# An attention and feed-forward kernel: TensorE's planned waits of the first stages filled with matmuls of the identity

## The chip, the cores and the metric

The kernel runs on one core of one Trainium2 chip. The metric is the device time of one execution in microseconds (us), as the median of several runs. Engines: PE (TensorE, matmuls, with its weight loads shown as PEld), DVE (VectorE), ACT (ScalarE), POOL (GpSimd) and SP (SyncE, which only issues transfers here). PE writes its results to PSUM, which this kernel uses as eight banks of 128 partitions by 2 KB.

## The reference

Linear attention with a decay per head runs in blocks of 64 positions for 4 batches, 8 heads, 768 positions and a head size of 64. Its output, laid out as 3072 rows of 512, goes through a feed-forward layer with SiLU.

```python
for b in range(nb):                                   # blocks of 64 positions
    intra = np.einsum('bhic,bhjc->bhij', qb, kb) * Dmask[None]   # lam ** (i - j), lower triangle
    intra = np.einsum('bhij,bhjd->bhid', intra, vb)
    inter = np.einsum('bhid,bhde->bhie', qb * lam_pow[None], kv_state)
    out[:, :, sl] = intra + inter
    kb_dec = kb * rev_pow[None]
    kv_state = lam_block[None, :, None, None] * kv_state + np.einsum('bhsd,bhse->bhde', kb_dec, vb)
...
h = x @ w_in                                          # 3072 x 512 times 512 x 2048
g = h * (1.0 / (1.0 + np.exp(-h)))
return g @ w_out                                      # 3072 x 2048 times 2048 x 512
```

## The kernel before

**Units and sets.** A unit is 128 positions (two blocks of 64) of one batch: 24 units, 6 along the sequence for each of 4 batches. Two units make a set, and q, k and v of a set are loaded by three transfers of 512 KB each from SP (`load_set`). The four first sets hold units 0 and 1 of one batch; later ones hold one unit of two batches.

**Attention of a set.** k is cast to bf16 (tile `kq`), q is scaled by the decay on its way to bf16 (`kq`, with `lam_q`), and v is scaled too (`vd`, with `lam_v`). Queries and keys are turned: in the first four sets by eight transposes on PE for each of k and q, which are matmuls against `ident` into the PSUM tile `tr` (L455), copied to SBUF as `kqT`; in later sets by a transposing DMA. PE then makes the state's increments (`d_ps`, L476 or L664) and the scores (`st_ps`, L527 or L674). DVE multiplies the scores by the triangle (`st`). PE makes the outputs from `st` and `vd` (`x_ps`, L551 or L696) and adds the part of the state (L556 or L704), after which `x_ps` is copied to `xt`, the feed-forward input, already transposed.

**Feed-forward.** The first product (`product1`, L843) makes `h_ps` from `w_in_bf` and `xt` in groups of eight matmuls of 128x256 or four of 128x512. SiLU on ACT (L852) turns `h_ps` into `g`. The second product is plain for eight units (L874) and otherwise a seven-product scheme with sums of operands made on DVE and POOL (L1087; L957 for the last group of the first product). Results go to DRAM from ACT's queue and, at the end, from SP's. The weights are loaded by POOL's queue in eight transfers, each held back until a load of k has landed (the copy to `gate`, L330).

**The planner.** No order is written out by hand. Every step is a `Task` with a key (its urgency), a planned duration on each engine that may run it, the tasks that it depends on, and the buffers that it uses (`Buf`, by pools; `bank` is a PSUM bank, eight of them). `Planner.order` plays a clock over the engines: at each event it gives every free engine the ready task with the least key whose buffers are free, and books `free[e] = now + t.on[e]`. A buffer's slot goes back to the end of its pool's list when its last user's planned end is reached, and a task takes its slot from the front of the list (`pop(0)`). Transfers are planned with rates (`SMALL`, `WIDE` and so on). What comes out is a list of tasks in planned order, and the kernel then issues the instructions in this order. So the order on each engine is fixed when the kernel is built; on the chip, each engine runs its own list in order, and semaphores hold an instruction until what it needs is there. If a planned duration is wrong, the order stays and the waits move.

`tile_of` makes a tile in the SBUF or PSUM slot that the planner chose; a new tile in a slot brings, at its first write, a wait for the last users of the tile that had the slot before.

`ident`, the identity matrix in bf16, is made by POOL at the start (L255, L256); the transposes of L455 use it.

## Time and profile before

| what | value |
|---|---|
| median of 3 runs | 208.56 us (208.56 to 210.06) |
| the profiled execution | 209.46 us, its span 207.8 us |
| PE busy | 187.7 us, 90% of the span, 2446 matmuls |
| DVE, ACT, POOL busy | 135.6, 110.4, 65.7 us |
| PE busy from 0 to 22.9 us | 10.74 us |
| PE busy from 28.61 us to the end | 172.10 of 179.19 us |
| DMA share, 0 to 22.9 us | 1.01 |

The span runs from the first to the last instruction of one execution; what lies around it makes the rest of that execution's time. Line numbers are those of the kernel before. A row of the timeline gives start, length, engine, line, operation, output from inputs, tile and shape, and in brackets the idle time before it with the instruction that ended it. A row of waits gives who waited for whom, in total, how often, and the longest. The ends of matmuls are modelled.

### The profile page before, as it was taken

To read this page: it belongs to the slowest core of one execution; us is meant where nothing else is said; L and a number is where in the kernel's file an instruction comes from. 1 tells how busy PE (TensorE), PEld (TensorE's weight loads), DVE (VectorE), ACT (ScalarE), POOL (GpSimd) and SP (SyncE) were. 2 spreads that over 40 slices of the span, in tenths; PEclk is the share of its full clock that TensorE was granted. 3 is DMA by queue.
4 is the path that set the end of the run, shared out by engine and by line. 5 is a ranking of instruction groups with operands and counts; after the bars stand their busy time and mean duration, and the time that the engine had idled before them with its cause. 6 is when DMAs were issued, how large, how long until landed. Compare 5 with 4: busy or idle time off the path is not lost.

```text
span 207.8 us, 5721 instructions
## 1 busy us (share of the span) xinstructions
PE 187.7 (90%) x2446; PEld 133.3 (64%) x2464; DVE 135.6 (65%) x234; ACT 110.4 (53%) x200; POOL 65.7 (32%) x86
## 2 busy tenths in 40 slices
PE   0258999999999999999997999997999999999993
PEld 0146679776667655544586745675476778888882
DVE  6469563787770186719999693899965854755511
ACT  3634666875444273457553286572646473666220
POOL 6222310623240042307666430477213222222200
PEclk9999999999999999999999999999999999999999
DMA  3999999999999999999979999911501110103303
GB/s 101 295 256 258 237 270 238 248 201 204 236 261 231 183 229 226 208 246 222 177 149 200 219 223 218 229 39 54 104 3 50 54 50 0 54 0 101 104 32 121
DMA packets 88617, 33.92 MB, mean 163 GB/s; under 512 B 67088, under 2 KB 87568, under 8 KB 88592
## 3 DMA queue, kind: packets, MB, share of 16 engines
q1 hardware_dynamic: 79232, 23.60, 56.2%
q0 software_dynamic: 4224, 4.19, 12.1%
q10 hardware_dynamic: 5136, 5.77, 8.3%
q8 instruction: 19, 0.31, 0.6%
q14 instruction: 6, 0.05, 0.1%
HBM read 27.27 MB, written 6.29 MB: 162 GB/s over the span
## 4 chain that ended last, share of the span: by engine, by line
PE 85%; DVE 7%; DMA 3%; ACT 2%; issue 1%; POOL 0%; DVEq 0%; POOLq 0%
PE h_ps L843 33%; PE o_ps L1087 21%; PE o_ps L874 13%; PE h_ps L957 6%; DMA raw<-in_k_dram 3%; PE tr L455 3%; PE x_ps L704 2%; DVE st L319 2%; PE d_ps L664 1%; PE x_ps L696 1%; DVE w_out_bf L319 1%; PE st_ps L674 1%; DVE kq L319 1%; PE x_ps L551 1%; PE d_ps L476 1%
## 5 line engine op out<-in xcount | busy, mean ns | idle before, releaser
L843 PE MATMUL h_ps<-xt,w_in_bf 128*128 128x256 bf16 (+1 forms) x441 | 75.8, 322 | 2.6 <-DVE xt L314 1.9
L852 ACT ACTIVATE g<-h_ps 128x512 bf16<-128x512 f32 x80 | 47.2, 595 | 33.8 <-PE h_ps L843 33.3
L843 PEld LDWEIGHTS <-w_in_bf 128*128 128x128 bf16 x448 | 43.7, 99 | 29.0 <-DVE xt L314 1.7
L319 DVE TENSOR_TENSOR st<-st_ps,tri 128x512 bf16<-128x512 f32 x32 | 20.3, 682 | 17.3 <-PE st_ps L674 17.2
L319 POOL TENSOR_TENSOR s<-g,s 128x512 bf16<-128x512 bf16 x16 | 19.2, 1198 | 39.2 <-DVE s L319 32.6
L874 PE MATMUL o_ps<-w_out_bf,g 128*128 128x512 bf16 x117 | 29.2, 379 | 0.7 <-issue 0.2
L1087 PEld LDWEIGHTS <-g 128*128 128x128 bf16 x256 | 24.9, 98 | 3.5
L1087 PEld LDWEIGHTS <-s 128*128 128x128 bf16 x192 | 18.7, 98 | 4.2 <-issue 1.4
L874 PEld LDWEIGHTS <-g 128*128 128x128 bf16 x128 | 12.1, 98 | 11.4
L319 DVE TENSOR_TENSOR osb<-o_ps,m 128x512 f32<-128x512 f32 (+1 forms) x15 | 8.7, 583 | 13.6 <-ACT m L312 8.8
L455 PE MATMUL tr<-ident,kq 128*128 128x128 bf16 x64 | 7.3, 264 | 10.3 <-POOL gate L330 6.9
L1087 PE MATMUL o_ps<-w_out_bf,s 128*128 128x256 bf16 x128 | 15.3, 273 | 1.2 <-DVE osb L319 1.2
L319 POOL TENSOR_TENSOR vd<-raw,lam_v 128x512 bf16<-128x512 f32 x10 | 13.8, 1386 | 6.5 <-DMA raw<-in_v_dram 6.3
L1087 PE MATMUL o_ps<-wsum,g 128*128 128x256 bf16 x128 | 15.1, 273 | 0.0
L1087 PE MATMUL o_ps<-w_out_bf,g 128*128 128x256 bf16 x128 | 14.8, 273 | 0.0
L312 ACT ACTIVATE xt<-x_ps 128x512 bf16<-128x512 f32 x15 | 9.2, 635 | 10.3 <-PE x_ps L704 6.1
L319 DVE TENSOR_TENSOR s<-g 128x512 bf16<-128x512 bf16 x16 | 10.5, 654 | 6.0 <-ACT g L852 4.0
L319 DVE TENSOR_TENSOR kq<-raw,lam_q 128x512 bf16<-128x512 f32 x17 | 13.7, 827 | 0.0
L455 PEld LDWEIGHTS <-kq 128*128 128x128 bf16 x64 | 5.3, 118 | 12.2 <-DVE kq L314 7.1
L312 ACT ACTIVATE m<-o_ps 128x512 f32<-128x512 f32 (+1 forms) x13 | 6.7, 514 | 11.7 <-PE o_ps L1087 11.7
L316 POOL CAST xe<-xf 64x256 bf16<-64x256 f32 (+1 forms) x8 | 6.5, 814 | 17.9 <-DVE xf L319 12.4
L312 ACT ACTIVATE osb<-o_ps 128x512 f32<-128x512 f32 (+1 forms) x12 | 6.7, 560 | 9.6 <-PE o_ps L874 4.8
(92 smaller groups left out, 245.6 us busy)
## 6 DMA issues: line engine op xcount, KB each, us to landing
raw<-in_k_dram SPq DMA_DIRECT2D x12, 512.0 KB, 7.6
raw<-in_q_dram SPq DMA_DIRECT2D x12, 512.0 KB, 8.3
raw<-in_v_dram SPq DMA_DIRECT2D x12, 512.0 KB, 7.0
out_dram<-osb ACTq DMA_DIRECT2D x20, 256.0 KB, 4.0
w_in_bf<-in_moe_w_in_dram POOLq DMA_DIRECT2D x4, 512.0 KB, 8.3
w_out_bf<-in_moe_w_out_dram POOLq DMA_DIRECT2D x4, 512.0 KB, 10.8
out_dram<-osb ACTq DMA_DIRECT2D x4, 128.0 KB, 1.8
out_dram<-osb SPq DMA_DIRECT2D x4, 128.0 KB, 1.7
```

The lines of the kernel that those rows point to most:

```text
L312: nc.scalar.activation(o, i, AF.Copy)
L316: nc.gpsimd.tensor_copy(o, i)
L319: (nc.vector if e == "DVE" else nc.gpsimd).tensor_tensor(o, a, b, op=op)
L455: nc.tensor.transpose(t[:, m, a], o.kq_of()[:, i, m, a], ident)
L476: nc.tensor.matmul(t[rp, m, :], lhsT=o.kq_of()[r, 0, m, a, p, :], rhs=o.vd_of()[r, 2 * m + p, a, :], start=m == 0 and a == 0, stop=True, s ...
L551: nc.tensor.matmul(t[rh, m], lhsT=o.vd_of()[r, 2 * m + h, a, :], rhs=o.st_of(h)[r, m, a], start=m == 0 and a == 0, stop=True, skip_group_c ...
L704: nc.tensor.matmul(x_of(c)[:, j, m, :], lhsT=o.xe[c].tile[:, (bs[0] + j) % 2, m, :], rhs=o.kqT_of()[:, 1, j, m, halves[c]], start=False, s ...
L843: nc.tensor.matmul(t[:, j, :], lhsT=w_in_bf[:, ko, 128 * (m1 + j):128 * (m1 + j) + 128], rhs=xt[gi].tile[:, ko, :], start=(ko == 0), stop= ...
L852: nc.scalar.activation(t[:, half * per:half * per + per], bank.tile, AF.Silu)
L874: nc.tensor.matmul(t, lhsT=g.tile[:, j, 128 * gp:128 * gp + 128], rhs=w_out_bf[:, ko, :], start=(ko == 0), stop=(ko == KO - 1))
L957: nc.tensor.matmul(t[:, j, :], lhsT=W[w]()[:, k2, f:f + 128], rhs=X(r)[:, k2, :], start=first and j == 0 and k2 == 0, stop=True, skip_grou ...
L1087: nc.tensor.matmul(t[:, i_, :], lhsT=src(j)[:, k2, 128 * r:128 * r + 128], rhs=W[w]()[:, 2 * j + k2, :], start=first and i_ == 0 and j == ...
```

## The change

The planner gets a `filler`, a function that makes a task of four matmuls of `ident` with `ident`, 128x128 each, into one PSUM bank. Nothing reads the result. Whenever, in the plan, PE is free between 1.7 and 30 us, finds no task to take, and more than two banks are free, it is given a filler: booked for 0.44 us before 6.0 us of the plan and for 0.22 us after. The filler takes the bank at the end of the list (`pop()`, the one freed last) and gives it back when its booked time is over. Because a filler occupies PE in the plan, later tasks can be placed differently, on all engines.

```diff
+    WARM, COLD = (1.7, 30.0), 6.0
...
+        self.filler = None
...
-        while len(out) < len(self.tasks):
+        fillers = 0
+        while len(out) < len(self.tasks) + fillers:
...
                 if took is None:
+
+                    if e == "PE" and self.filler and self.WARM[0] <= now < self.WARM[1] and len(self.pools["bank"]) > 2:
+                        b = Buf("bank")
+                        b.slot = self.pools["bank"].pop()
+                        free[e] = now + (0.44 if now < self.COLD else 0.22)
+                        seq += 1
+                        heapq.heappush(release, (free[e], seq, b))
+                        heapq.heappush(events, free[e])
+                        out.append((now, len(out), e, self.filler(b)))
+                        fillers += 1
                     continue
...
+    def filler(b):
+        def go(e):
+            t = tile_of(b, [128, 4, 128], F32, "ones")
+            for i in range(4):
+                nc.tensor.matmul(t[:, i, :], lhsT=ident, rhs=ident, start=i == 0, stop=True, skip_group_check=True)
+
+        return Task("filler", {"PE": 0.22}, go, [], [])
+
+    plan.filler = filler
```

## The prediction

> **What bounds the kernel now.** I read the page first, then TensorE's waits, then its timeline over the first 40 us.

> ```profile
> span 207.8 us, 5721 instructions
> PE 187.7 (90%) x2446; PEld 133.3 (64%) x2464; DVE 135.6 (65%) x234; ACT 110.4 (53%) x200; POOL 65.7 (32%) x86
> PE   0258999999999999999997999997999999999993
> PEclk9999999999999999999999999999999999999999
> PE 85%; DVE 7%; DMA 3%; ACT 2%; issue 1%; POOL 0%; DVEq 0%; POOLq 0%
> ```

> TensorE (PE) is the bound: 90% busy, 85% of the chain, and almost without a gap from the fourth slice on. Whatever delays the end of its first stages delays the kernel. Its waits lie nearly all at the start:

> ```profile
> PE tr L455 <- POOL gate L330: 6.9, 1, 6.9
> PE tr L455 <- DVE kq L319: 2.1, 2, 1.7
> PE h_ps L843 <- DVE xt L314: 1.9, 2, 1.0
> PE d_ps L476 <- DVE vd L319: 1.4, 1, 1.4
> PE o_ps L1087 <- DVE osb L319: 1.2, 1, 1.2
> PE tr L455 <- ACT kq L312: 1.2, 3, 0.6
> ```

> (The 6.9 us end with the first cast of k, which ends at 6.83; the gate copy is only the last to start.) After 38 us only the 1.2 and one 1.0 are left. Then PE's timeline: start, length, operation, count.

> ```profile
> 6.88 1.26 PE L455 MATMUL tr<-ident,kq 128*128 128x128 bf16 x8 [6.88 <-POOL gate L330]
> ...
> 18.97 1.86 PE L843 MATMUL h_ps<-xt,w_in_bf 128*128 128x256 bf16 x8 [0.91 <-DVE xt L314]
> 20.63 1.06 PE L455 MATMUL tr<-ident,kq 128*128 128x128 bf16 x8
> 21.49 1.76 PE L843 MATMUL h_ps<-xt,w_in_bf 128*128 128x256 bf16 x8
> 23.18 0.45 PE L476 MATMUL d_ps<-vd,kq 64*64 64x64 bf16 x32
> 23.45 0.62 PE L527 MATMUL st_ps<-kqT 64*64 64x128 bf16 x32
> 24.01 1.05 PE L843 MATMUL h_ps<-xt,w_in_bf 128*128 128x256 bf16 x8
> ...
> 31.23 0.61 PE L455 MATMUL tr<-ident,kq 128*128 128x128 bf16 x8
> 31.68 5.40 PE L843 MATMUL h_ps<-xt,w_in_bf 128*128 128x256 bf16 x48
> 37.01 0.44 PE L476 MATMUL d_ps<-vd,kq 64*64 64x64 bf16 x32
> 37.29 0.62 PE L527 MATMUL st_ps<-kqT 64*64 64x128 bf16 x32
> ```

> Eight h_ps matmuls take 1.86 us at 18.97 and 1.05 us at 24.01; eight transposes 1.06 and later 0.61. The pace doubles at about 23.0 us, after 4.0 us without a gap (18.97 to 23.0), although the PEclk row shows 9 from the start: that row does not show this state, the durations do. So there are two things to win early, idle time (13.0 us before 28.6) and half speed.

> **The change, part by part.** It adds 58 fillers of four 128x128 matmuls, 232 with as many weight loads. In the order in which the changed program's instructions stand on PE they form eight runs of 15, 10, 5, 12, 5, 1, 7 and 3: ahead of the first transposes of k, then of q, then of the first d_ps, and so on to the sixth group of transposes.

> *Price of one filler.* The plan books 0.44 us before 6.0 and 0.22 after, which is pace alone: transposes of the same shape start every (1.06-0.31)/7 = 0.107 us slow and (0.61-0.22)/7 = 0.056 fast. But each filler takes the bank that was freed last, so in a run all have the same bank, and the program says what follows: 50 of the 58 (all but the first of each run) wait, at their first matmul, for PE's own semaphore, which the filler directly before raises with its last matmul. In the kernel before, PE's waits on itself reach back 21 matmuls or more, so nothing was ever waited for. No row shows such a wait; it is bounded by these:

> ```profile
> L455 PE MATMUL tr<-ident,kq x48: 219/311/314, 6.9 to 31.6; 128*128 128x128 bf16 x48
> ...
> 9.15 1.28 DVE L319 TENSOR_TENSOR kq<-raw,lam_q 128x512 bf16<-128x512 f32 x2
> 10.49 0.93 PE L455 MATMUL tr<-ident,kq 128*128 128x128 bf16 x7 [0.31 <-DVE kq L319]
> ```

> A matmul of this shape lasts 0.22 us fast, 0.31 slow, and PE starts 0.06 after the instruction that releases it (10.43 to 10.49). A linked filler is then 3 x 0.056 + 0.22 + 0.055 = 0.443 us fast and 3 x 0.107 + 0.31 + 0.055, with a first step of 0.08 as at 10.49, = 0.66 slow. From below: 0.22 if the wait costs nothing; from above: 0.53 fast, with the 0.14 us that h_ps took at 18.97 after xt's end at 18.83. I take 0.443, since the rows that it is made of are of this shape and engine.

> *Sum.* I compare the end of the third st_ps group, 37.91 us before (37.29 + 0.62). By then PE had done 104 matmuls of L843; in the new order it has done 88 there, otherwise the same work, so the point to compare with is 37.9 - 16 x 0.109 = 36.2. After the change:
> - ident is there at 1.38, first filler at 1.4;
> - fillers at full pace: 50 x 0.443 + 8 x 0.224 = 24.0;
> - slow start: if 4.0 us of activity double the pace as at 23.0, six fillers run slow, 6 x 0.22 = 1.3;
> - real work at full pace: 88 x 0.109 = 9.6, 48 transposes x 0.056 = 2.7, three pairs d_ps and st_ps of 0.83 (23.18 to 24.01) = 2.5, two pairs of x_ps of 0.98 (26.21 to 27.19) = 2.0: 16.8;
> - the last matmul's end, 0.2.

> That makes 43.7, later by 7.5 us. No wait for data is in it, and few are left: the first transposes come at about 9.2 instead of 6.88, with k cast by 7.2; the second at about 13.9, while the copies and the scaling between (0.6 + 0.42 + 1.28 after 9.7) end at 12.0. Each stage of DVE and ACT that waits for transposes or scores begins as late as PE brings them. The fillers take 25.3 us where the plan gave 10 x 0.44 + 48 x 0.22 = 15.0, more than the 13.0 idle microseconds and what full speed saves.

> Given back later: of the two waits after 38 us (2.2 us) I take half, 1.1, since DVE's side work then has 7 us more lead; bounds 0 and 2.2. Net +6.4.

> *The rest.* The plan deals the work out anew: DVE stands at 233 operations (234 before), ACT and POOL exchange a few copies, SP issues one transpose ahead of one v load instead of behind it. Each queue issues the same transfers. Cost nothing, hidden under a PE that is 97% busy from 40 us on; without that cover 2 us either way. The weights of the 232 matmuls load beside them, at the same pace (seven in 0.39 us at 25.71).

> The profiled execution took 209.46 us (span 207.8), the median is 208.56: 215.9 for a profiled one, **215.0** by the median.

> [...]

> **The rivals.**
> 1. *The pace stays slow much longer.* In a linked slow filler the array is fed 0.43 of 0.66 us, 65%. In the trace, 15.1 to 19.0 was not enough: eight transposes, 0.85 us of feeding, and x_ps, 1.26, make 2.1 in 3.9 us, 54%; the 100% from 18.97 on was enough. If fillers do not count, only the first 16 h_ps with d_ps and st_ps behind them (over 4 us unbroken) release it, with 48 fillers past: 42 more slow ones, 9.2 us, and real work at half pace, 4.4: 208.56 + 6.4 + 13.6 = 228. Released half way, at some 16 us, it costs 2 to 4: 217 to 219. For it: 65 lies nearer to 54 than to 100; against: counted until its last result is out, a filler is busy for 0.60 of 0.66. [...]
> 2. *The other side: the wait on its own semaphore hardly costs.* If the mark comes back before the array is empty, a filler is its pace, 0.22: 10.9 us less than 24.0, the point comes at about 33, and the waits for DVE and ACT return, so that at best some 2 to 3 us are won: 206 to 207. It decides below 0.443 - 6.4/50 = 0.32 us a filler. Against: ACT's copy after the first transposes starts at 8.18, with the last of them ending at 8.14, so the mark comes at the end.
> 3. *The late start is absorbed.* PE is idle for 7.0 us after 40 (2.15 to 130, 4.88 behind), and if these were waits for transfers, 209 would come out. Against: PE's wait list names no DMA, and only 2.2 us of waits for others there.

> **How the numbers follow.** Forecast 0.50 (its own range 211.5 to 218.5: 0.41 to 0.50 us a filler, 4 to 7 slow microseconds, 0 to 2.2 given back); rival 1 0.33, from 217 to 228; rival 2 0.10; rival 3 0.07. The range, 211 to 227, leaves out rival 2, most of rival 3 and the top of rival 1. A measurement here can tell about 1%: rival 2 is half beyond it (faster 0.05) and half within, with most of rival 3 (same 0.10); the rest is slower, 0.85.

> **What would show it.** Right: fillers of a run 0.41 to 0.50 us apart once their matmuls come every 56 ns, with a gap before every fourth; first transposes at 9 to 10 us; third st_ps group ending near 43.7; the later stretch as long as before within 2 us. Wrong: fillers 0.25 us apart; first transposes before 7.5; matmuls still every 107 ns past 12 us (rival 1); a third st_ps group as late as said with the end at 209 (rival 3).

## The result, and the profile after

The changed kernel takes 218.34 us (median of 6 runs, 217.58 to 218.41) against 208.78 us of the kernel before in 6 runs: 1.0436 times, with a 95% interval of 1.0404 to 1.0468. The forecast was 215.0, in a range of 211 to 227.

The page of the profile after, in the lines that answer to those shown of before (execution 218.41 us):

```profile
span 216.7 us, 6181 instructions
PE 206.7 (95%) x2679; PEld 148.5 (69%) x2696; DVE 134.2 (62%) x233; ACT 111.9 (52%) x204; POOL 61.5 (28%) x83
PE   6999999999999999999999999999999999999993
PE 90%; DVE 4%; issue 2%; ACT 1%; DMA 1%; DVEq 0%; POOL 0%; POOLq 0%; ACTq 0%
L1179 PE MATMUL ones<-ident 128*128 128x128 bf16 x232 | 26.1, 244 | 4.5 <-POOL ident L269 1.4
```

The gaps of the first slices are gone, PE is 95% busy instead of 90%, and the kernel is 4% slower: busy with the wrong thing. The last line is the fillers, 26.1 us of PE. (Line numbers have moved: L843 is now L856, L455 L468, L527 L540.) TensorE's waits after:

```profile
PE ones L1179 <- POOL ident L269: 1.4, 1, 1.4
PE o_ps L1100 <- DVE osb L332: 0.4, 1, 0.4
PE o_ps L887 <- issue: 0.3, 2, 0.2
PE h_ps L856 <- ACT xt L325: 0.2, 1, 0.2
```

No real work waits for data any more in the first 46 us. A list of waits like this would look like a success. The fillers' waits on PE itself do not stand in it, since a matmul counts as busy until its modelled end. They show with the weight loads, where the profile names no release and puts them down to "issue", 50 times, 9.7 us in all:

```profile
PEld L1179 <- issue: 9.7, 50, 0.2
```

They also show in the timeline, in the time that a run of fillers takes for its count:

```profile
1.44 9.57 PE L1179 MATMUL ones<-ident 128*128 128x128 bf16 x60 [1.44 <-POOL ident L269]
10.80 1.06 PE L468 MATMUL tr<-ident,kq 128*128 128x128 bf16 x8
11.65 5.19 PE L1179 MATMUL ones<-ident 128*128 128x128 bf16 x40
16.68 0.61 PE L468 MATMUL tr<-ident,kq 128*128 128x128 bf16 x8
17.13 2.15 PE L1179 MATMUL ones<-ident 128*128 128x128 bf16 x20
...
29.24 1.91 PE L856 MATMUL h_ps<-xt,w_in_bf 128*128 128x256 bf16 x16
...
46.10 0.62 PE L540 MATMUL st_ps<-kqT 64*64 64x128 bf16 x32
```

The first transposes start at 10.80 instead of 6.88 us, and at half pace (1.06 us); at 16.68 the pace is full (0.61). The third st_ps group ends at 46.72 us. Within a run, the trace has a linked filler (one that waits for the filler before it) every 0.64 us slow and every 0.44 us fast; the step from the fourth matmul to the next filler's first is 367 ns slow and 275 fast, where others are 107 and 55. The starts change from 107 to 55 ns apart at 14.26 us.

### The profile page after: what moved, and what is told of

It reads as the page before. It is cut to its first block, busy times and chain, and to the rows that moved or that the text cites. A ratio compares the mean times of both kernels' runs of the same rounds, so it can differ in the third digit from the quotient of the medians.

```text
span 216.7 us, 6181 instructions
## 1 busy us (share of the span) xinstructions
PE 206.7 (95%) x2679; PEld 148.5 (69%) x2696; DVE 134.2 (62%) x233; ACT 111.9 (52%) x204; POOL 61.5 (28%) x83
## 4 chain that ended last, share of the span: by engine, by line
PE 90%; DVE 4%; issue 2%; ACT 1%; DMA 1%; DVEq 0%; POOL 0%; POOLq 0%; ACTq 0%
PE h_ps L856 32%; PE o_ps L1100 20%; PE ones L1179 12%; PE o_ps L887 10%; PE h_ps L970 6%; PE x_ps L717 2%; PE tr L468 2%; PE d_ps L677 1%; PE st_ps L687 1%; PE x_ps L564 1%; PE x_ps L709 1%; DMA out_dram<-osb 1%; PE d_ps L489 1%; DVE w_out_bf L332 1%; DVE xf L332 1%
## 5 line engine op out<-in xcount | busy, mean ns | idle before, releaser
L856 PE MATMUL h_ps<-xt,w_in_bf 128*128 128x256 bf16 (+1 forms) x440 | 74.2, 317 | 0.6 <-ACT xt L325 0.2
L865 ACT ACTIVATE g<-h_ps 128x512 bf16<-128x512 f32 x80 | 46.6, 596 | 26.8 <-PE h_ps L856 26.0
L856 PEld LDWEIGHTS <-w_in_bf 128*128 128x128 bf16 x448 | 43.1, 98 | 25.3 <-issue 0.7
L1179 PE MATMUL ones<-ident 128*128 128x128 bf16 x232 | 26.1, 244 | 4.5 <-POOL ident L269 1.4
L1179 PEld LDWEIGHTS <-ident 128*128 128x128 bf16 x232 | 18.3, 110 | 11.4 <-issue 9.7
L887 PEld LDWEIGHTS <-g 128*128 128x128 bf16 x128 | 12.2, 98 | 12.1
L329 POOL CAST xe<-yf 64x512 bf16<-64x512 f32 x6 | 4.3, 722 | 45.9 <-DVE yf L332 45.9
L325 ACT ACTIVATE xt<-x_ps 128x512 bf16<-128x512 f32 x16 | 9.9, 647 | 13.9 <-PE x_ps L717 10.0
L1100 PE MATMUL o_ps<-wsum,g 128*128 128x256 bf16 x128 | 15.1, 273 | 0.0
L332 DVE TENSOR_TENSOR s<-g 128x512 bf16<-128x512 bf16 x16 | 9.5, 594 | 6.4 <-ACT g L865 4.5
L332 POOL TENSOR_TENSOR vd<-raw,lam_v 128x512 bf16<-128x512 f32 x10 | 13.0, 1304 | 0.2
L325 ACT ACTIVATE kqT<-tr 128x512 bf16<-128x512 bf16 x9 | 5.3, 602 | 14.5 <-PE tr L468 14.2
L325 ACT ACTIVATE m<-o_ps 128x512 f32<-128x512 f32 (+1 forms) x13 | 6.7, 513 | 10.6 <-PE o_ps L1100 10.2
```

The source lines that it names most:

```text
L325: nc.scalar.activation(o, i, AF.Copy)
L329: nc.gpsimd.tensor_copy(o, i)
L332: (nc.vector if e == "DVE" else nc.gpsimd).tensor_tensor(o, a, b, op=op)
L856: nc.tensor.matmul(t[:, j, :], lhsT=w_in_bf[:, ko, 128 * (m1 + j):128 * (m1 + j) + 128], rhs=xt[gi].tile[:, ko, :], start=(ko == 0), stop= ...
L865: nc.scalar.activation(t[:, half * per:half * per + per], bank.tile, AF.Silu)
L887: nc.tensor.matmul(t, lhsT=g.tile[:, j, 128 * gp:128 * gp + 128], rhs=w_out_bf[:, ko, :], start=(ko == 0), stop=(ko == KO - 1))
```

## The experiments

Each was timed against the kernel before on the same chip; that kernel had a median of 209.18 us in the first four and 209.22 in the last three. The edits are made in the changed kernel unless it is said otherwise, and "..." stands for lines left out.

**One tile for a run of fillers.** Order and matmuls as changed, without PE's waits on itself.

```diff
-            t = tile_of(b, [128, 4, 128], F32, "ones")
+            t = held.get(b.slot) or tile_of(b, [128, 4, 128], F32, "ones")
+            held[b.slot] = t
...
+        if e == "PE" and t.key != "filler":
+            held.clear()
         t.fn(e)
```

> The order and all 232 filler matmuls of the change stay; a run of fillers now shares one PSUM tile, so that the 50 waits of PE on its own semaphore are gone. Theory (the loss is these waits, 0.44 us a linked filler instead of 0.22, and the slow clock that they keep until 14.2 us): matmuls of a run every 56 ns once fast, no gap before every fourth, fast pace from about 5.4 us (4.0 us after the first filler), the third st_ps group ends at 34 to 37 us instead of 46.7, and 206 to 209 us in all. Rival (232 more matmuls on PE and the new plan cost by themselves): 214 us or more.

Measured: 208.18 us, ratio 0.995 (0.9931 to 0.9969). Timeline of PE:

```profile
1.43 5.50 PE L1182 MATMUL ones<-ident 128*128 128x128 bf16 x60 [1.43 <-POOL ident L269]
6.85 0.90 PE L468 MATMUL tr<-ident,kq 128*128 128x128 bf16 x8
...
14.77 1.56 PE L1182 MATMUL ones<-ident 128*128 128x128 bf16 x25 [0.65 <-issue]
...
27.98 0.21 PE L564 MATMUL x_ps<-st,vd 64*64 64x128 bf16 x1 [1.49 <-issue]
...
36.41 0.62 PE L540 MATMUL st_ps<-kqT 64*64 64x128 bf16 x32
```

The same 60 matmuls take 5.50 us instead of 9.57; the pace doubles at 5.6 us; the third st_ps group ends at 37.03 us, 9.7 earlier. So the 50 waits are the loss: (1.0436 - 0.995) x 209 = 10.2 us. They come from a new tile in the bank that the filler before has just used; fillers that take another bank were not tried. The stops of 0.65 and 1.49 us with no release were not expected.

**The new order without fillers.**

```diff
     for _, _, e, t in plan.order():
-        t.fn(e)
+        if t.key != "filler":
+            t.fn(e)
```

> The order that the changed plan gives, with the filler instructions left out of it. Theory (the new order is about as good as the old): 208 to 211 us, slow pace until 20 to 25 us as in the kernel before. Rival (the new order itself is worse): 214 us or more, the third st_ps group no earlier than 42 us.

Measured: 207.57 us, ratio 0.9915 (0.9895 to 0.9935). The theory's range just missed on the good side: the order as such wins 1.8 us. PE's waits in this run:

```profile
PE tr L468 <- POOL gate L343: 7.0, 1, 7.0
PE tr L468 <- DVE kq L332: 3.2, 4, 1.7
PE h_ps L856 <- DMA w_in_bf<-in_moe_w_in_dram: 1.0, 1, 1.0
PE tr L468 <- ACT kq L325: 0.6, 2, 0.4
PE o_ps L1100 <- DVE osb L332: 0.4, 1, 0.4
PE x_ps L717 <- issue: 0.3, 1, 0.3
```

Of the two late waits of before (1.2 for osb and 1.0 for xt) 0.4 us is left, without PE being any later. Against this run the free-running fillers of the one above cost about 0.35% (0.995 to 0.9915; the two intervals touch), and win nothing.

**The old order, with a warm start only.** In the kernel before, ahead of the loop that issues the tasks:

```diff
-    for _, _, e, t in plan.order():
+    order = plan.order()
+    warm = ps.tile([128, 4, 128], F32, tag="bank7", name="ones")
+    for i in range(60):
+        nc.tensor.matmul(warm[:, i % 4, :], lhsT=ident, rhs=ident, start=i % 4 == 0, stop=True, skip_group_check=True)
+    for _, _, e, t in order:
```

> The kernel before in its own order, with 60 matmuls of the identity into one PSUM tile ahead of everything on PE, none of them waiting for another. They end at 1.4 + 4.0 + 23 x 0.056 = 6.7 us, about when the first transposes can start. Theory (the early clock is worth something by itself, the stages after it are half TensorE): fast pace from 5 to 6 us on and kept, 206 to 207.5 us. Rival (the start is bound by DVE and ACT, the pace hardly matters): 208 to 208.8 us with matmuls every 56 ns at 10 us. Second rival (the gaps of the first stages lose the clock again): matmuls every 107 ns somewhere between 10 and 19 us.

Measured: 209.17 us, ratio 1.0002 (0.9985 to 1.002): no difference, and no sign of the theory's 206 to 207.5. The second rival holds, while at 10.05 us the fast pace was still there:

```profile
10.05 0.56 PE L455 MATMUL tr<-ident,kq 128*128 128x128 bf16 x7 [0.37 <-DVE kq L319]
10.65 0.32 PE L476 MATMUL d_ps<-vd,kq 64*64 64x64 bf16 x16
12.36 0.41 PE L476 MATMUL d_ps<-vd,kq 64*64 64x64 bf16 x16 [1.39 <-DVE vd L319]
12.54 1.08 PE L527 MATMUL st_ps<-kqT 64*64 64x128 bf16 x32
```

The pace doubles at 5.6 us, is still full at 10.65 (0.32 where 0.43 was) and half again at 12.54 (1.08 as before), although the longest stop in between is 1.75 us (7.7 to 9.45). It stays half until about 22.7 us; in the kernel before it was half until 23.0.

**Half the links.** Two fillers share a tile: against the run with one tile for a run of fillers, the tile is taken out of `held` when it is used a second time.

```diff
-            t = held.get(b.slot) or tile_of(b, [128, 4, 128], F32, "ones")
-            held[b.slot] = t
+            t = held.pop(b.slot, None)
+            if t is None:
+                t = held[b.slot] = tile_of(b, [128, 4, 128], F32, "ones")
```

> The change with two fillers to a tile, so that 24 waits on PE's own semaphore are left of 50; PE is fed 0.85 of 1.07 us, 80%, while slow. Theory (each link costs 0.22 us, and the clock is let go by the share of time in which the array is fed, between the 67% that did not do it and the 77% of the window that did): 26 x 0.22 = 5.7 us less, fast pace from 5 to 9 us on, another 1 to 2 us less: 210.5 to 212 us. Rival (only feeding without a break counts): slow pace until the first transposes or later, 212 to 213.5 us.

Measured: 210.2 us, ratio 1.0049 (1.003 to 1.0068), 0.3 us below the theory's range; the pace doubles at 5.7 us. The gap after a link is as long as in the change, only rarer: the first 60 matmuls take 6.66 us, and four slow and three and a half fast pairs with the gaps of the change (367 and 275 ns) come to 6.64. So in this run breaks of that length did not hold the pace back. At 80% fed (0.85 of 1.07 us) it doubled 4.3 us after the first filler, where 67% (0.43 of 0.64 us) in the changed kernel had not brought it in 9 us. The theory's 67% and 77% are that kernel's, from 1.44 to 10.80 and from 10.80 to 14.26 us; that a share between them decides was the author's estimate and is not shown.

**Twice the links.** A new tile for every two matmuls:

```diff
-            t = tile_of(b, [128, 4, 128], F32, "ones")
             for i in range(4):
...
+                if i in (0, 2):
+                    b.tile = None
+                    t = tile_of(b, [128, 4, 128], F32, "ones")
...
```

> The change with a new PSUM tile for every two filler matmuls instead of every four: the same 232 matmuls, 108 waits of PE on its own semaphore instead of 50. Theory (each such wait adds a fixed price, 0.22 us fast and about 0.21 slow, and the clock goes by the fed share): two matmuls every 0.33 us fast and 0.43 slow; fed 0.21 of 0.43 us, 50%, less than the 67% that was not enough, so the slow pace lasts to the first h_ps; 58 x 0.22 = 12.8 us more, and 5 to 8 for the longer slow pace: 235 to 240 us. Rival (the price goes with the matmuls and not with the waits): 218 to 220 us. Rival on the clock (any activity releases it within 15 us): 230 to 233 us.

Measured: 240.36 us, ratio 1.1489 (1.147 to 1.1508), 0.4 us above the theory's range. Two matmuls come every 0.43 us slow and 0.33 fast, as worked out. Two lines on either side of the first h_ps:

```profile
46.09 1.06 PE L468 MATMUL tr<-ident,kq 128*128 128x128 bf16 x8
...
58.94 0.61 PE L468 MATMUL tr<-ident,kq 128*128 128x128 bf16 x8
```

Half pace lasts into the first 16 h_ps and ends at 50.6 us. With 0, 24, 50 and 108 links there are 208.2, 210.2, 218.3 and 240.4 us for the same 232 matmuls: the price rises with the links, and faster in the two runs in which the pace stayed slow for long (to 14.26 and 50.6 us). It is not one price per link: 24 of them at 0.22 us would be 5.3 us and cost 2.0, in part because that run has no stops of 2.1 us without a release, as the run without links has.

**Fillers cut to the measured waits.** One tile for a run, and at most so many fillers:

```diff
+    held, runs, CAP = {}, [0, 0], (15, 8, 2, 3, 3, 0, 0, 0)
...
+            runs[1] += 1
+            if runs[1] > CAP[runs[0]]:
+                return
+            t = held.get(b.slot) or tile_of(b, [128, 4, 128], F32, "ones")
+            held[b.slot] = t
...
```

> The order of the change, no waits of PE on itself, and only as many fillers as the measured waits of the run without fillers hold: runs of 15, 8, 2, 3, 3 and none after the sixth stage (31 of 58). Theory A (idle time and slow pace of the first stages are worth what they last): fast pace from 5.6 us on and kept, first h_ps at 17 instead of 18.8 us, 205 to 206.5 us. Theory B (from the first h_ps on the loads of w_in set the pace, the fourth lands at 33.3 to 34.5 us in every run without long delays): first h_ps at 17, longer waits of h_ps for w_in, third st_ps group again at 35 to 36 us, 206.8 to 208 us against 208.8 to 209.2 of the kernel before.

Measured: 208.25 us, ratio 0.9937 (0.9913 to 0.996): no better than the order without fillers, and above the ranges of both theories. First PE's timeline, then DVE's:

```profile
17.70 0.23 PE L468 MATMUL tr<-ident,kq 128*128 128x128 bf16 x1 [1.77 <-DVE kq L332]
...
18.71 3.40 PE L856 MATMUL h_ps<-xt,w_in_bf 128*128 128x256 bf16 x16
...
35.20 1.05 PE L856 MATMUL h_ps<-xt,w_in_bf 128*128 128x256 bf16 x8 [1.13 <-DMA w_in_bf<-in_moe_w_in_dram]
```

```profile
16.96 1.29 DVE L332 TENSOR_TENSOR kq<-raw,lam_q 128x512 bf16<-128x512 f32 x2 [1.70 <-DMA raw<-in_q_dram]
```

The mechanism is that of theory B, transfers that set the pace, but it bites earlier than B said, and the third st_ps group ends later (37.07 us instead of 35 to 36): the second set's q lands at 16.9 us, so its transposes and the h_ps behind them come at 17.7 and 18.71 (18.78 in the run without fillers), however fast PE was before. Then h_ps waits for the fourth part of w_in, which lands at 35.2 instead of 33.3 to 34.5. That the fast pace would be kept, as theory A said, failed: after that stop of 1.77 us the first h_ps run slow, as 3.40 us for 16 shows.

**Wide fillers.** One tile for a run, each filler one matmul of 512 columns:

```diff
-            for i in range(4):
-                nc.tensor.matmul(t[:, i, :], lhsT=ident, rhs=ident, start=i == 0, stop=True, skip_group_check=True)
...
+            nc.tensor.matmul(t, lhsT=ident, rhs=ident[:, None, :].to_broadcast([128, 4, 128]), start=True, stop=True, skip_group_check=True)
```

> As the run in which all fillers of a run share one tile, but each filler is one matmul of 512 columns instead of four of 128: the same time on the array (0.213 us fast, 0.427 slow), a quarter of the instructions. Theory (the two stops of 0.65 and 1.49 us in that run, which ended with no release, are PE's instructions coming in late, since it used up 464 more within 30 us): no stop over 0.5 us put down to issue before 30 us, the third st_ps group ends at 35 to 36.5 us instead of 37.0, 207 to 208 us. Rival (the stops are something else): they stay, 208 us and more.

Measured: 207.14 us, ratio 0.99 (0.9882 to 0.9918), the best of all, though its interval overlaps that of the order without fillers.

```profile
18.59 1.91 PE L856 MATMUL h_ps<-xt,w_in_bf 128*128 128x256 bf16 x16
...
34.93 0.62 PE L540 MATMUL st_ps<-kqT 64*64 64x128 bf16 x32
```

No stop is put down to issue, and the third st_ps group ends at 35.55 us, 1.5 earlier than with four times the instructions. That fits instructions arriving late, but does not show it. The pages of the run with four times the instructions and of the run with half the links list the same transfers of instructions (21 with 0.34 MB and 6 with 0.05 MB), and only the first run has such stops. The cause stays open. The pace is full from the start of h_ps on (1.91 us for 16), and still the third st_ps group ends only 0.4 us ahead of the run without fillers (35.95). That is all that the early clock is worth here.

## Why the prediction was right, and where its size was off

*Mechanism.* The forecast named the wait of each filler on the one before it, in the same bank. The runs with 0, 24, 50 and 108 of these waits show that they are the cause.

*Price of a linked filler.* 0.443 us fast and 0.66 slow were forecast from the length of a transpose, the pace and the lag of a release; 0.44 and 0.64 were measured. Rival 2 (the wait costs next to nothing) falls with it.

*The slow start* is the term that was mis-sized. Forecast: 4.0 us of activity, six slow fillers, 1.3 us. Measured: slow until 14.26 us, 19 fillers, 19 x (0.64 - 0.44) = 3.8, and eight slow transposes, 1.06 - 0.61 = 0.45. That is 3.0 us more, all of the difference at the third st_ps group (46.72 against 43.7). No run shows the upper end of the "4 to 7 slow microseconds" in the forecast's own range; the start was slow for 12.8 us (1.44 to 14.26). The step that failed is the reading of "4.0 us of activity": at 23.0 us PE had been fed all the time, the fillers feed it 0.43 of 0.64 us. What came is the middle form of rival 1, release at some 16 us and 217 to 219 us, to which the forecast's own sum should have given more weight. The trace's record of the clock begins at 14.28 us. From the first transposes to the doubling (10.80 to 14.26 us) PE was fed about 77% of the time, from 1.44 to 10.80 about 67% (estimates from the starts of the matmuls, 107 ns for each); from 10.4 to 12.1 us a filler, the eight transposes and another filler follow each other without a break. That this stretch made the difference is argued, not tried. In the runs that fed PE 80% or more from the first filler on (1.43 or 1.44 us) the pace doubled between 5.3 and 6.7 us, but 9 us at 67% and 46 us at 50%, with denser pieces between, did not bring it. After 14.26 us the pace of the changed kernel stayed full at a fed share of 0.22 of 0.44 us, half the time; in the run with twice the links the same share, 0.21 of 0.43 us, did not bring it.

*Given back.* 1.1 us were forecast for PE's later lateness; 10.5 us at the common point (46.72 - 36.2) became 8.9 at the end of the span, 1.6 back. The size was near, but by luck, for the reason was wrong: the run in the new order without fillers is not late and has lost the same waits (2.2 to 0.4 us). So the new order takes them away, without any lateness of PE.

*The rest.* "Cost nothing, 2 us either way" for the new order: it wins 1.8 us of 209. Which step of it does so was not taken apart. *Rival 3* (the lateness is absorbed) is refuted by the 8.9 us that stay.

So the loss is the sum of three measured pieces, in shares of the time before: the order -0.85%, 232 matmuls at pace with the two stops that came with them +0.35%, the waits on itself with the slow clock +4.9%. With the wide fillers, which bring no such stops, the second piece is not seen (0.99 against 0.9915).

## What to carry to other kernels

Work that is put into waits has to be checked for waits of its own: here a new tile in the bank that was freed last made each linked filler wait for the last matmul of the one before, and doubled its price (0.44 instead of 0.22 us). Price a group by pace plus, for each link, the last matmul's full length and the release (here 3 x 0.056 + 0.22 + 0.055 = 0.443 us, where 0.44 was measured), not by pace alone. And before filling a wait, ask what ends it: in the new order without fillers the later ones ended with transfers (q at 16.7 us, w_in at 27 and 34 us), and neither a busy PE nor a fast one brought the third st_ps group forward by more than 0.4 us.

## What the runs showed of the hardware that was not expected

The profile's mean granted clock, 0.975 to 1.00 in these runs, does not show the slow start: it is 1.00 for the first 22.9 us of the kernel before, where matmuls came every 107 ns. In the traces of the kernels before and after, the record of the clock begins with the doubling, at 22.97 and 14.28 us, and the time before it stands as full. What the prediction says of the PEclk row holds for that time alone. A later loss does stand in the row, as in the warm start alone:

```profile
PEclk9975899999999999999999999999999999999999
```

The 7, 5 and 8 cover 10.4 to 25.9 us, and the half pace in them lasted from about 12.4 to about 22.7 (d_ps takes 0.41 us for 16 at 12.36 and 0.49 us for 32 at 22.51).

And the stops of 0.65 and 1.49 us, put down to issue, came in the run with 232 fillers' matmuls of 128 columns and no waits of PE on itself; with 58 matmuls of 512 columns they were gone. What they are was not shown.
